# Reordering the head and the attention bursts of a fused attention and feed-forward kernel

## The chip, the cores and the metric

The kernel runs on one core of a Trainium2 chip. The metric is the device time of one execution in microseconds (us). One core has five engines that matter here: TensorE (matmul; PE in the profile, and PEld for its weight loads), VectorE (DVE), ScalarE (ACT), GpSimd (POOL, which here only issues loads that cast from f32 to bf16), and SyncE (SP, which here issues the stores of the output and the transposing transfers). Matmul results land in PSUM, eight banks of 128 x 512 f32; ACT and DVE read them out from there.

## The reference

The input is q, k, v of 8 batches x 12 heads x 448 positions x 64, and the weights of a feed-forward layer, 768 to 2048 to 768, with a slope alpha for each of the 2048.

```python
def _attn_ref(q, k, v):                       # (8, 12, 448, 64)
    scores = (1.0 / np.sqrt(64)) * np.matmul(q, k.transpose(0, 1, 3, 2))
    attn = np.maximum(scores, 0.0) ** 2 / 448
    return np.matmul(attn, v)

def _moe_ref(x, w_in, w_out, alpha):          # (3584, 768), (768, 2048), (2048, 768), (2048,)
    h = x @ w_in
    g = np.maximum(h, 0.0) + alpha * np.minimum(h, 0.0)
    return g @ w_out

# x is the attention output with the heads side by side: (8 * 448, 12 * 64)
```

## The kernel before

The work is cut into 24 "quads" of four heads (three quads to a batch) and each quad into seven "chunks" of 64 key positions. A chunk is four 64x64 matmuls into a pair of PSUM banks (`score_mm`), a relu out of PSUM on ACT or DVE, and a square in bf16 from SBUF to SBUF on DVE. When the seven chunks of a quad are squared, `attnv` multiplies them with v (28 matmuls). After three quads a batch has its input to FFN1 (`f1`: 16 outputs `ff`, six matmuls each over `km`, then `neg` on ACT and a multiply-add on DVE). Two batches share one FFN2 (`f2`: 7 row blocks `c` x 2 halves, 16 matmuls each, a copy out on ACT and two stores). The scores of later quads are mixed in between these. q and k are transposed either on TensorE (`turn_pe`, quads 0 to 5) or by a copy on DVE and a transposing transfer (`turn_dma`, from quad 6). Each engine works through its instructions in the order of this program; `take_pair` and `take_bank` hand out the PSUM banks that were taken longest ago.

```python
    raw_pool = ctx.enter_context(tc.tile_pool(name="raw", bufs=3))
    v_pool = ctx.enter_context(tc.tile_pool(name="v", bufs=7))
    perm_pool = ctx.enter_context(tc.tile_pool(name="perm", bufs=2))
    T_pool = ctx.enter_context(tc.tile_pool(name="T", bufs=4))
    rl_pool = ctx.enter_context(tc.tile_pool(name="rl", bufs=7))
    at_pool = ctx.enter_context(tc.tile_pool(name="at", bufs=12))
    xT_pool = ctx.enter_context(tc.tile_pool(name="xT", bufs=2))
    g_pool = ctx.enter_context(tc.tile_pool(name="g", bufs=1))
    neg_pool = ctx.enter_context(tc.tile_pool(name="neg", bufs=3))
    o_pool = ctx.enter_context(tc.tile_pool(name="o", bufs=4))
    # ... [cut: weights, identity, PSUM tile]
    def take_pair():
        lo = min((0, 2, 4, 6), key=lambda i: (max(taken[i], taken[i + 1]), i))
        take(lo, 2)
        return psum[:, lo:lo + 2]

    def take_bank():
        i = min(range(8), key=lambda i: (taken[i], i))
        take(i, 1)
        return psum[:, i]
    # ... [cut: loads; quad 0 is loaded ahead of the rest as f32 and cast on DVE and ACT]
    def turn_pe(n, cuts=((0, NJ, "D"),), cuts_k=((0, NJ, "D"),)):
        t = T_pool.tile([128, 2, NJ, 128], BF16, tag="T", name="T")
        for i, name in enumerate("qk"):
            src = raw.pop((n, name))
            for lo, hi, eng in (cuts, cuts_k)[i]:
                ps = take_bank().bitcast(BF16)
                for j in range(lo, hi):
                    for s in range(2):
                        nc.tensor.transpose(ps[64 * s:64 * s + 64, 128 * j:128 * j + 128], src[:, s, j], ident)
                dst = t[:, i, lo:hi].rearrange("p j c -> p (j c)")
                if eng == "D":
                    nc.vector.tensor_copy(dst, ps[:, 128 * lo:128 * hi])
                else:
                    nc.scalar.copy(dst, ps[:, 128 * lo:128 * hi])
        T[n] = t
    def turn_dma(n):
        p = perm_pool.tile([128, 2, NJ, 2, D], BF16, tag="perm", name="perm")
        for i, name in enumerate("qk"):
            nc.vector.tensor_copy(p[:, i], raw.pop((n, name)).rearrange("p s j d -> p j s d"))
        t = T_pool.tile([128, 2, NJ, 128], BF16, tag="T", name="T")
        nc.sync.dma_start_transpose(out=t.rearrange("p a j c -> p (a j) c"),
                                    in_=p.rearrange("p a j s d -> p (a j s d)"))
        T[n] = t
    def score_mm(n, j):
        ps = take_pair()
        t = T[n]
        for r in range(2):
            for c in range(2):
                nc.tensor.matmul(ps[64 * c:64 * c + 64, r, :S],
                                 t[64 * r:64 * r + 64, 1, j, 64 * c:64 * c + 64],
                                 t[64 * r:64 * r + 64, 0, :, 64 * c:64 * c + 64],
                                 start=True, stop=True)
        return ps

    def relu(ps, eng):
        rl = rl_pool.tile([128, 2, S], BF16, tag="rl", name="rl")
        if eng == "A":
            nc.scalar.activation(rl, ps[:, :, :S], ACTF.Relu)
        else:
            nc.vector.tensor_scalar(rl, ps[:, :, :S], 0.0, None, ALU.max)
        return rl

    def square(n, j, rl):
        a = at_pool.tile([128, 2, S], BF16, tag="at", name="at")
        nc.vector.tensor_tensor(a, rl, rl, ALU.mult)
        att[(n, j)] = a

    def attnv(n):
        ps = take_pair()
        vv = vraw.pop(n)
        for j in range(NJ):
            a = att.pop((n, j))
            for r in range(2):
                for s in range(2):
                    nc.tensor.matmul(ps[64 * s:64 * s + 64, r, :S],
                                     vv[64 * r:64 * r + 64, s, j, :],
                                     a[64 * r:64 * r + 64, s],
                                     start=(j == 0), stop=(j == NJ - 1))
        b, g = divmod(n, NG)
        if g == 0:
            xT[b] = xT_pool.tile([128, NG, 2, S], BF16, tag="xT", name="xT")
        if n < 2:
            nc.scalar.activation(xT[b][:, g], ps[:, :, :S], ACTF.Copy, scale=out_scale)
            return
        nc.scalar.activation(xT[b][:, g, 0], ps[:, 0, :S], ACTF.Copy, scale=out_scale)
        nc.vector.tensor_scalar(xT[b][:, g, 1], ps[:, 1, :S], out_scale, None, ALU.mult)

    late = []

    def sc(chunks):

        for n, j, eng in chunks:
            late.append((n, j, relu(score_mm(n, j), eng)))

    def sq(k=99):
        for g in late[:k]:
            square(*g)
        del late[:k]

    def run(chunks):
        sc(chunks)
        sq()
    def f1_mm(ps, b, ff, ks):
        for km in ks:
            nc.tensor.matmul(ps, w_in_sb[:, km // 2, km % 2, bass.ts(ff, 128)],
                             xT[b][:, km // 2, km % 2, :],
                             start=(km == 0), stop=(km == KM - 1))

    def f1_out(ps, b, ff):
        if b % 2 == 0 and ff == 0:
            gT[b // 2] = g_pool.tile([128, KF, 2 * S], BF16, tag="g", name="gT")
        neg = neg_pool.tile([128, S], F32, tag="neg", name="neg")
        nc.scalar.activation(neg, ps, ACTF.Relu, scale=-1.0)
        nc.vector.scalar_tensor_tensor(gT[b // 2][:, ff, (b % 2) * S:(b % 2) * S + S],
                                       neg, beta_sb[:, ff:ff + 1], ps, ALU.mult, ALU.add)
        sq(1)

    def f1(b, ff):
        ps = take_bank()[:, :S]
        f1_mm(ps, b, ff, range(KM))
        f1_out(ps, b, ff)

    def f2(sb, c, hf, parts=((0, HALF),)):
        o = o_pool.tile([128, HALF], F32, tag="o", name="osb")
        for lo, hi in parts:
            ps = take_bank()[:, :hi - lo]
            for ff in range(KF):
                nc.tensor.matmul(ps, gT[sb][:, ff, bass.ts(c, 128)], w_out_sb[:, hf, ff, lo:hi],
                                 start=(ff == 0), stop=(ff == KF - 1))
            nc.scalar.copy(o[:, lo:hi], ps)
            for u in range(2):
                blk = 2 * c + u
                b, j = 2 * sb + blk // NJ, blk % NJ
                rows = out[b * S:(b + 1) * S].rearrange("(pp j) d -> j pp d", j=NJ)
                eng = nc.scalar if u and hi - lo < HALF else nc.sync
                eng.dma_start(out=rows[j][:, hf * HALF + lo:hf * HALF + hi], in_=o[64 * u:64 * u + 64, lo:hi])
    # ... [the schedule: the head]
    pat = "ADAAAAA"

    def ch(n, lo, hi, p=pat):
        return [(n, j, p[j]) for j in range(lo, hi)]
    load_w_in(0)
    load_w_in(1)
    turn_pe(0, ((0, 4, "D"), (4, NJ, "D")), ((0, 2, "D"), (2, NJ, "D")))
    sc(ch(0, 0, 4))
    sq(3)
    load_qk(3)
    load_v(3)
    sc(ch(0, 4, 6))
    turn_pe(1)
    sc(ch(0, 6, 7))
    sq(4)
    load_w_in(2)
    load_w_in(3)
    sc(ch(1, 0, 3, "AAA"))
    attnv(0)
    load_qk(4)
    load_v(4)
    sq(2)
    sc(ch(1, 3, 4))
    turn_pe(2)
    sq(1)
    sc([(1, 4, "D"), (1, 5, "A"), (1, 6, "A")])
    sq(2)
    load_w_out(0)
    sc(ch(2, 0, 2, "AA"))
    sq(2)
    attnv(1)
    load_qk(5)
    load_v(5)
    load_w_out(1)
    sc(ch(2, 2, 4, "AAAAAAA"))
    nc.vector.tensor_scalar(beta_sb, alpha_sb, -1.0, 1.0, ALU.mult, ALU.add)
    sq(3)
    sc(ch(2, 4, 7, "AAAAADA"))
    sq()
    early = []
    for ff in range(2):
        ps = take_bank()[:, :S]
        f1_mm(ps, 0, ff, range(4))
        early.append(ps)
    attnv(2)
    for ff in range(2):
        f1_mm(early[ff], 0, ff, range(4, KM))
        f1_out(early[ff], 0, ff)
    def prepare(n):
        if n < NQ:
            turn_dma(n)
        if n + 2 < NQ:
            load_qk(n + 2)
            load_v(n + 2)
    # ... [cut: FFN1 of batch 0 with the chunks of quads 3 and 4, FFN2 c=0..2, quads 4 and 5]
    def some(k):
        lo = at_c[0]
        at_c[0] = min(lo + k, len(chunks))
        return [(n, j, e) for (n, j), e in zip(chunks[lo:at_c[0]], "ADA")]

    def burst(n):

        sc(some(3))
        attnv(n)
        sc(some(3))
        sq()
    for ff in range(KF):
        if ff < 4:
            f1_mm(early[ff], 1, ff, range(4, KM))
            f1_out(early[ff], 1, ff)
        else:
            f1(1, ff)
        if ff in (1, 5, 9):
            prepare(6 + ff // 4)
    f2(0, 3, 0)
    run(some(3))
    f2(0, 3, 1)
    f2(0, 0, 1)
    run(some(3))
    f2(0, 1, 1)
    run(some(3))
    f2(0, 2, 1)
    f2(0, 4, 0)
    prepare(9)
    burst(6)
    f2(0, 4, 1)
    f2(0, 5, 0)
    burst(7)
    f2(0, 5, 1)
    f2(0, 6, 0)
    prepare(10)
    burst(8)
    f2(0, 6, 1)

    for b in range(2, B):
        n0 = NG * (b + 1)
        last = b == B - 1
        sb = b // 2
        for ff in range(KF):
            if not last and ff == 8:
                run(some(3))
                prepare(n0 + 2)
            f1(b, ff)
        if b % 2 == 0:
            units = [(sb, c, h) for c in range(3) for h in range(2)]
            at = {1: 0, 3: 1, 5: 2}
        else:
            units = [(sb, c, h) for c in range(3, 7) for h in range(2)]
            at = {1: 0, 4: 1, 7: 2}
        for i, u in enumerate(units):
            if i in at and not last:
                g = at[i]
                if g != 1:
                    prepare(n0 + 3 + g // 2)
                burst(n0 + g)
            if last and i == len(units) - 1:
                f2(*u, parts=((0, 256), (256, HALF)))
            else:
                f2(*u)
```

## Time and profile before

| what | before |
|---|---|
| time of three runs, median (lowest to highest) | 392.98 us (392.55 to 398.75) |
| span of the profiled execution | 389.5 us |
| mean granted TensorE clock | 1.000 |
| busy share: PE, PEld, DVE, ACT, POOL | 97%, 55%, 68%, 53%, 17% |
| FFN2 matmuls (line 252) | 912, mean 323 ns in the record |
| FFN1 matmuls (line 229) | 768, mean 353 ns |
| relu on ACT (line 178), on DVE (line 180) | 120 of 928 ns, 48 of 1086 ns |
| square on DVE (line 185) | 168 of 618 ns |
| multiply-add of FFN1 on DVE (line 238), `neg` on ACT (line 237) | 128 of 678 ns, 128 of 546 ns |
| transposing transfers | 18, median 7.6 us from issue to landing |
| share of the DMA engines by stretches of 10 us | 0.99 to 1.30 up to 90 us, 0.00 to 1.20 after |

How to read it. A matmul's record runs from its start to a modelled end, and the next one starts long before that end; so the mean duration of a record is not what the matmul costs, and a PE that is busy for 97% is not a PE at its peak. What a stretch of matmuls costs is read from one start to the next in the timeline or in the chain of work that ended last. In the rows of groups, a name such as `rl<-psum` says which tile is written from which, `x120` how often; after the bar stand the engine's busy time in them, the mean duration of one in ns, and the idle time of that engine just before them with what ended it. A line of the timeline has the start, the time to the end of the last of the merged instructions, engine, line, operation, tiles and count. "idle before <-X" in brackets says that the engine had stood still and that X released it.

### The profile page before, as it was taken

The numbers are of one execution on the slowest core, as the hardware profiler recorded it, in microseconds if no ns is written. First come the engines' busy times: TensorE is split into PE (matmuls) and PEld (weight loads), VectorE is DVE, ScalarE is ACT, GpSimd is POOL, SyncE is SP. The second block draws the span as 40 slices with busy tenths as digits, with TensorE's granted clock in tenths as the row PEclk, the third lists the DMA queues.
The fourth block names the chain that finished last, engine by engine and source line by source line (L and its number), as shares of the span: only waits on it lengthen the run. The fifth ranks groups of instructions, "written<-read, shape, count | busy, mean of one in ns | idle before, by whom it ended". The sixth has DMA issues, their size and how long they took to land.

```text
span 389.5 us, 7956 instructions
## 1 busy us (share of the span) xinstructions
PE 378.2 (97%) x3228; PEld 216.0 (55%) x3228; DVE 263.9 (68%) x418; ACT 207.5 (53%) x332; POOL 65.5 (17%) x97
## 2 busy tenths in 40 slices
PE   7779999999999999999999999999999999999996
PEld 5435454555665556645655456654666546655564
DVE  3977966865777777868756687878756786735300
ACT  4966566545546546555455554655644565524311
POOL 7557212520202040202202022102000000000000
PEclk9999999999999999999999999999999999999999
DMA  9999999996859089574939259490832311120023
GB/s 181 191 202 204 206 211 206 167 195 139 134 86 144 29 129 169 82 98 73 159 89 146 55 53 176 95 153 8 164 82 51 80 24 46 42 61 2 12 72 82
DMA packets 71909, 43.75 MB, mean 112 GB/s; under 512 B 38208, under 2 KB 71872, under 8 KB 71872
## 3 DMA queue, kind: packets, MB, share of 16 engines
q0 software_dynamic: 27312, 23.04, 40.4%
q1 hardware_dynamic: 44128, 19.65, 25.7%
q8 instruction: 25, 0.41, 0.4%
q10 hardware_dynamic: 432, 0.56, 0.4%
q14 instruction: 12, 0.10, 0.1%
HBM read 47.00 MB, written 11.01 MB: 149 GB/s over the span
## 4 chain that ended last, share of the span: by engine, by line
PE 88%; ACT 5%; DVE 3%; issue 2%; DMA 1%; ACTq 0%
PE psum L252 38%; PE psum L229 36%; PE psum L169 7%; PE psum L195 6%; ACT rl L178 4%; DVE at L185 2%; DMA qfirst<-in_q_dram 1%; DVE T L147 1%; PE psum L144 1%; ACT xT L205 1%; DVE rl L180 1%; DVE gT L238 0%; ACT osb L254 0%; DVE qraw L127 0%; ACTq L260 0%
## 5 line engine op out<-in xcount | busy, mean ns | idle before, releaser
L252 PE MATMUL psum<-w_out_sb,gT 128*128 128x384 bf16 (+2 forms) x912 | 150.7, 323 | 0.2
L229 PE MATMUL psum<-xT,w_in_sb 128*128 128x448 bf16 x768 | 148.7, 353 | 1.1 <-ACT xT L205 0.6
L252 PEld LDWEIGHTS <-gT 128*128 128x128 bf16 x912 | 87.6, 98 | 61.5 <-issue 6.7
L229 PEld LDWEIGHTS <-w_in_sb 128*128 128x128 bf16 x768 | 74.2, 98 | 71.8 <-issue 4.4
L238 DVE SCALAR_TENSOR_TENSOR gT<-neg,beta_sb,psum 128x448 bf16<-128x448 f32 x128 | 84.5, 678 | 41.3 <-ACT neg L237 40.9
L237 ACT ACTIVATE neg<-psum 128x448 f32<-128x448 f32 x128 | 69.3, 546 | 70.3 <-PE psum L229 64.7
L178 ACT ACTIVATE rl<-psum 128x896 bf16<-128x896 f32 x120 | 102.9, 928 | 1.2 <-PE psum L169 1.2
L185 DVE TENSOR_TENSOR at<-rl 128x896 bf16<-128x896 bf16 x168 | 94.1, 618 | 3.5 <-ACT rl L178 3.4
L254 ACT COPY osb<-psum 128x384 f32<-128x384 f32 (+2 forms) x57 | 27.0, 474 | 97.5 <-PE psum L252 94.0
L180 DVE TENSOR_SCALAR rl<-psum 128x896 bf16<-128x896 f32 x48 | 52.1, 1086 | 37.1 <-PE psum L169 37.1
L91 POOL DMA_DIRECT2D qraw<-in_q_dram x24 | 17.2, 718 | 190.2 <-DVE perm L155 170.1
L169 PE MATMUL psum<-T 64*64 64x448 bf16 x672 | 44.7, 355 | 3.8 <-DVE T L147 1.4
L195 PE MATMUL psum<-at,vraw 64*64 64x448 bf16 x672 | 37.9, 351 | 0.7 <-ACT rl L178 0.2
L169 PEld LDWEIGHTS <-T 64*64 64x64 bf16 x672 | 20.9, 105 | 21.6 <-issue 14.6
L195 PEld LDWEIGHTS <-vraw 64*64 64x64 bf16 x672 | 24.8, 106 | 10.9 <-issue 3.7
L206 DVE TENSOR_SCALAR xT<-psum 128x448 bf16<-128x448 f32 x22 | 13.7, 625 | 14.3 <-PE psum L195 7.2
L91 POOL DMA_DIRECT2D kraw<-in_k_dram x24 | 17.3, 721 | 6.9 <-PE psum L169 3.3
L98 POOL DMA_DIRECT2D vraw<-in_v_dram x25 | 18.0, 722 | 1.2 <-DMA w_in_sb<-in_moe_w_in_dram 0.4
L205 ACT ACTIVATE xT<-psum 128x448 bf16<-128x448 f32 x22 | 12.0, 545 | 5.4 <-PE psum L195 5.4
L155 DVE COPY perm<-qraw 128x896 bf16<-128x896 bf16 x18 | 11.0, 612 | 0.4 <-DMA T<-perm 0.4
L108 POOL DMA_DIRECT2D w_in_sb<-in_moe_w_in_dram x16 | 10.0, 628 | 7.4 <-DMA vraw<-in_v_dram 2.5
L155 DVE COPY perm<-kraw 128x896 bf16<-128x896 bf16 x18 | 11.0, 609 | 0.0
(19 smaller groups left out, 35.5 us busy)
## 6 DMA issues: line engine op xcount, KB each, us to landing
out_dram<-osb SPq DMA_DIRECT2D x110, 96.0 KB, 2.3
vraw<-in_v_dram POOLq DMA_DIRECT2D x25, 224.0 KB, 7.4
qraw<-in_q_dram POOLq DMA_DIRECT2D x24, 224.0 KB, 4.8
kraw<-in_k_dram POOLq DMA_DIRECT2D x24, 224.0 KB, 6.7
w_in_sb<-in_moe_w_in_dram POOLq DMA_DIRECT2D x16, 192.0 KB, 8.7
w_out_sb<-in_moe_w_out_dram POOLq DMA_DIRECT2D x2, 1536.0 KB, 18.6
qfirst<-in_q_dram SPq DMA_DIRECT2D x1, 448.0 KB, 4.4
kfirst<-in_k_dram ACTq DMA_DIRECT2D x1, 448.0 KB, 4.7
```

The source lines that it names most:

```text
L91: nc.gpsimd.dma_start(out=t.rearrange("p m j d -> p m (j d)"), in_=flat[:, 2 * g:2 * g + 2])
L155: nc.vector.tensor_copy(p[:, i], raw.pop((n, name)).rearrange("p s j d -> p j s d"))
L169: nc.tensor.matmul(ps[64 * c:64 * c + 64, r, :S], t[64 * r:64 * r + 64, 1, j, 64 * c:64 * c + 64], t[64 * r:64 * r + 64, 0, :, 64 * c:64 * ...
L178: nc.scalar.activation(rl, ps[:, :, :S], ACTF.Relu)
L180: nc.vector.tensor_scalar(rl, ps[:, :, :S], 0.0, None, ALU.max)
L185: nc.vector.tensor_tensor(a, rl, rl, ALU.mult)
L195: nc.tensor.matmul(ps[64 * s:64 * s + 64, r, :S], vv[64 * r:64 * r + 64, s, j, :], a[64 * r:64 * r + 64, s], start=(j == 0), stop=(j == NJ ...
L229: nc.tensor.matmul(ps, w_in_sb[:, km // 2, km % 2, bass.ts(ff, 128)], xT[b][:, km // 2, km % 2, :], start=(km == 0), stop=(km == KM - 1))
L237: nc.scalar.activation(neg, ps, ACTF.Relu, scale=-1.0)
L238: nc.vector.scalar_tensor_tensor(gT[b // 2][:, ff, (b % 2) * S:(b % 2) * S + S], neg, beta_sb[:, ff:ff + 1], ps, ALU.mult, ALU.add)
L252: nc.tensor.matmul(ps, gT[sb][:, ff, bass.ts(c, 128)], w_out_sb[:, hf, ff, lo:hi], start=(ff == 0), stop=(ff == KF - 1))
L254: nc.scalar.copy(o[:, lo:hi], ps)
```

## The change

The change has five parts, and the arithmetic stays as it was.

1. **Head.** The first of the two copies that take the transposed k of quad 0 out of PSUM goes from DVE to ACT; the read-out of the second attention result (quad 1) is split between ACT and DVE as it already is for later quads; one square of quad 2 is done on ACT; three instead of two chunks of quad 2 come ahead of the A@V of quad 1; and the first four instead of the first two outputs of FFN1 are begun early, over the 512 rows of `w_in` whose input is there before quad 2 is finished. They stand half before and half after the A@V of quad 2, in PSUM banks that `hold` keeps out of the rotation until they are read. This is to keep ACT and DVE evenly loaded and TensorE at work while they catch up.
2. **Bursts.** A burst between two FFN2 blocks had three chunks, A@V, three chunks; now it has three, A@V, two.
3. **Plain triples.** The chunks that the bursts give up are done as a second plain group of three under each FFN1 (at outputs 6 and 12; before, one group at 8), and as a fourth plain group in the FFN2 of batch 0.
4. **Quad 8.** It was loaded twice; now it is loaded once.
5. **Transposing transfers.** `turn_dma` and the loads are called sooner, so that the transposed tiles are there for the earlier chunks.

```diff
@@ -75,6 +75,12 @@
         take(lo, 2)
         return psum[:, lo:lo + 2]
 
+    def hold():
+
+        i = min(range(8), key=lambda i: (taken[i], i))
+        taken[i] = 10**9
+        return i
+
     def take_bank():
         i = min(range(8), key=lambda i: (taken[i], i))
         take(i, 1)
@@ -180,9 +186,12 @@
             nc.vector.tensor_scalar(rl, ps[:, :, :S], 0.0, None, ALU.max)
         return rl
 
-    def square(n, j, rl):
+    def square(n, j, rl, eng="D"):
         a = at_pool.tile([128, 2, S], BF16, tag="at", name="at")
-        nc.vector.tensor_tensor(a, rl, rl, ALU.mult)
+        if eng == "A":
+            nc.scalar.activation(a, rl, ACTF.Square)
+        else:
+            nc.vector.tensor_tensor(a, rl, rl, ALU.mult)
         att[(n, j)] = a
 
     def attnv(n):
@@ -199,7 +208,7 @@
         b, g = divmod(n, NG)
         if g == 0:
             xT[b] = xT_pool.tile([128, NG, 2, S], BF16, tag="xT", name="xT")
-        if n < 2:
+        if n == 0:
             nc.scalar.activation(xT[b][:, g], ps[:, :, :S], ACTF.Copy, scale=out_scale)
             return
         nc.scalar.activation(xT[b][:, g, 0], ps[:, 0, :S], ACTF.Copy, scale=out_scale)
@@ -231,7 +240,7 @@
                              start=(km == 0), stop=(km == KM - 1))
 
     def f1_out(ps, b, ff):
-        if b % 2 == 0 and ff == 0:
+        if b // 2 not in gT:
             gT[b // 2] = g_pool.tile([128, KF, 2 * S], BF16, tag="g", name="gT")
         neg = neg_pool.tile([128, S], F32, tag="neg", name="neg")
         nc.scalar.activation(neg, ps, ACTF.Relu, scale=-1.0)
@@ -267,7 +276,7 @@
 
     load_w_in(0)
     load_w_in(1)
-    turn_pe(0, ((0, 4, "D"), (4, NJ, "D")), ((0, 2, "D"), (2, NJ, "D")))
+    turn_pe(0, ((0, 4, "D"), (4, NJ, "D")), ((0, 2, "A"), (2, NJ, "D")))
     sc(ch(0, 0, 4))
     sq(3)
     load_qk(3)
@@ -289,46 +298,58 @@
     sc([(1, 4, "D"), (1, 5, "A"), (1, 6, "A")])
     sq(2)
     load_w_out(0)
-    sc(ch(2, 0, 2, "AA"))
-    sq(2)
+    early = {}
+    todo = []
+
+    def some_early(count):
+        for ff, km in todo[:count]:
+            if ff not in early:
+                early[ff] = hold()
+            f1_mm(psum[:, early[ff], :S], 0, ff, (km,))
+        del todo[:count]
+
+    sc(ch(2, 0, 3, "AAA"))
+    sq(3)
     attnv(1)
     load_qk(5)
     load_v(5)
     load_w_out(1)
-    sc(ch(2, 2, 4, "AAAAAAA"))
+    todo = [(ff, km) for ff in range(4) for km in range(4)]
+    sc(ch(2, 3, 4, "AAAAAAA"))
     nc.vector.tensor_scalar(beta_sb, alpha_sb, -1.0, 1.0, ALU.mult, ALU.add)
-    sq(3)
+    sq(2)
     sc(ch(2, 4, 7, "AAAAADA"))
+    some_early(8)
+    square(*late.pop(-2), "A")
     sq()
-    early = []
-    for ff in range(2):
-        ps = take_bank()[:, :S]
-        f1_mm(ps, 0, ff, range(4))
-        early.append(ps)
     attnv(2)
-    for ff in range(2):
-        f1_mm(early[ff], 0, ff, range(4, KM))
-        f1_out(early[ff], 0, ff)
+    some_early(8)
+    for ff in range(4):
+        f1_mm(psum[:, early[ff], :S], 0, ff, range(4, KM))
+        f1_out(psum[:, early[ff], :S], 0, ff)
+        take(early[ff], 1)
 
 
     def f1s(b, lo, hi):
         for ff in range(lo, hi):
             f1(b, ff)
 
+    def load(n):
+        if n < NQ:
+            load_qk(n)
+            load_v(n)
+
     def prepare(n):
         if n < NQ:
             turn_dma(n)
-        if n + 2 < NQ:
-            load_qk(n + 2)
-            load_v(n + 2)
-
-    f1s(0, 2, 3)
+        load(n + 2)
+
     turn_pe(3)
     load_qk(6)
     load_v(6)
-    f1s(0, 3, 5)
+    f1s(0, 4, 6)
     sc(ch(3, 0, 3))
-    f1s(0, 5, 8)
+    f1s(0, 6, 8)
     sc(ch(3, 3, 6))
     f1s(0, 8, 10)
     turn_pe(4)
@@ -368,7 +389,7 @@
 
         sc(some(3))
         attnv(n)
-        sc(some(3))
+        sc(some(2))
         sq()
 
     early = []
@@ -384,25 +405,29 @@
             f1_out(early[ff], 1, ff)
         else:
             f1(1, ff)
-        if ff in (1, 5, 9):
-            prepare(6 + ff // 4)
+        if ff in (1, 4, 7):
+            turn_dma(6 + ff // 3)
+        if ff == 11:
+            load(9)
+            load(10)
     f2(0, 3, 0)
     run(some(3))
     f2(0, 3, 1)
     f2(0, 0, 1)
+    prepare(9)
     run(some(3))
     f2(0, 1, 1)
     run(some(3))
     f2(0, 2, 1)
+    run(some(3))
     f2(0, 4, 0)
-    prepare(9)
     burst(6)
     f2(0, 4, 1)
     f2(0, 5, 0)
+    prepare(10)
     burst(7)
     f2(0, 5, 1)
     f2(0, 6, 0)
-    prepare(10)
     burst(8)
     f2(0, 6, 1)
 
@@ -411,9 +436,10 @@
         last = b == B - 1
         sb = b // 2
         for ff in range(KF):
-            if not last and ff == 8:
+            if not last and ff in (6, 12):
                 run(some(3))
-                prepare(n0 + 2)
+            if not last and ff in (1, 9):
+                prepare(n0 + 2 + ff // 8)
             f1(b, ff)
         if b % 2 == 0:
             units = [(sb, c, h) for c in range(3) for h in range(2)]
@@ -424,8 +450,8 @@
         for i, u in enumerate(units):
             if i in at and not last:
                 g = at[i]
-                if g != 1:
-                    prepare(n0 + 3 + g // 2)
+                if g == 1:
+                    prepare(n0 + 4)
                 burst(n0 + g)
             if last and i == len(units) - 1:
                 f2(*u, parts=((0, 256), (256, HALF)))
```

## The prediction

> **What bounds the kernel now.** I read the page first, then the chain of work that ended last in order of time, then the busy time by stages, and last the timeline of the two places that the change touches.
>
> ```profile
> PE 378.2 (97%) x3228; PEld 216.0 (55%) x3228; DVE 263.9 (68%) x418; ACT 207.5 (53%) x332; POOL 65.5 (17%) x97
> PE 88%; ACT 5%; DVE 3%; issue 2%; DMA 1%; ACTq 0%
> PE psum L252 38%; PE psum L229 36%; PE psum L169 7%; PE psum L195 6%; ACT rl L178 4%; DVE at L185 2%; DMA qfirst<-in_q_dram 1%; DVE T L147 1%; PE psum L144 1%; ACT xT L205 1%; DVE rl L180 1%; DVE gT L238 0%; ACT osb L254 0%; DVE qraw L127 0%; ACTq L260 0%
> ```
>
> TensorE sets the end: 88% of the chain is matmuls, and the two feed-forward layers alone are 74%. None of these matmuls is removed. What the change can win is the other 12%, and within the 88% whatever PE loses when it turns from one kind of matmul to another. So I need the cost of a matmul, from the chain in order of time:
>
> ```profile
> 66.38 16.75 PE psum L229 x88
> 131.66 0.69 PE psum L169 x12
> 189.76 7.97 PE psum L252 x48
> ```
>
> FFN1: 16.75/88 = 0.190 us each. FFN2: 7.97/48 = 0.166 us with the turns, 2.60 us for a block of 16 in the undisturbed middle. A plain triple of chunks (12 matmuls) takes 0.69 us, of which some 0.1 is the turn back to full-size matmuls. Then the stages, with PE, DVE and ACT side by side:
>
> ```profile
> 7.20:31.00 23.80, 18.70 (x277) 10.11 (x278) 20.56 (x36) 18.48 (x24) 13.80 (x22) 1.00 1.24 198
> 31.00:49.20 18.20, 17.92 (x149) 8.60 (x146) 15.44 (x26) 12.44 (x21) 8.37 (x12) 1.00 1.29 204
> 213.70:256.70 43.00, 43.00 (x362) 24.88 (x360) 33.91 (x54) 24.19 (x39) 6.42 (x9) 1.00 0.63 100
> ```
>
> Only from 7.2 to 31 us is PE idle by its records (18.70 of 23.80 us), and there DVE (20.56) and ACT (18.48) are nearly full: the head is bound by relu and square. In the later periods PE never rests, and DVE has 9 us of air in 43.
>
> The timeline of the head's end shows the waits:
>
> ```profile
> 19.81 0.38 PE L195 MATMUL psum<-at,vraw 64*64 64x448 bf16 x4
> 20.24 0.92 ACT L203 ACTIVATE xT<-psum 128x896 bf16<-128x896 f32 x1 [0.33 <-PE psum L195]
> 21.06 3.34 ACT L178 ACTIVATE rl<-psum 128x896 bf16<-128x896 f32 x4
> 22.54 1.08 DVE L180 TENSOR_SCALAR rl<-psum 128x896 bf16<-128x896 f32 x1
> 22.83 1.67 PE L229 MATMUL psum<-xT,w_in_sb 128*128 128x448 bf16 x8 [0.43 <-ACT rl L178]
> 23.54 2.22 DVE L185 TENSOR_TENSOR at<-rl 128x896 bf16<-128x896 bf16 x4
> 24.43 1.77 PE L195 MATMUL psum<-at,vraw 64*64 64x448 bf16 x28
> 26.23 0.54 ACT L205 ACTIVATE xT<-psum 128x448 bf16<-128x448 f32 x1 [1.83 <-PE psum L195]
> 26.82 2.05 PE L229 MATMUL psum<-xT,w_in_sb 128*128 128x448 bf16 x10 [0.63 <-ACT xT L205]
> ```
>
> ACT stands 0.33 us for the A@V of quad 1, then reads it out whole, and only then begins four relus of quad 2; DVE squares the last four after that; the A@V of quad 2 waits for them; and FFN1 waits 0.63 us for its read-out. And a burst, in a later period:
>
> ```profile
> 237.31 0.80 PE L169 MATMUL psum<-T 64*64 64x448 bf16 x12
> 237.51 0.54 ACT L205 ACTIVATE xT<-psum 128x448 bf16<-128x448 f32 x1
> 238.11 5.36 PE L252 MATMUL psum<-w_out_sb,gT 128*128 128x384 bf16 x32
> ```
>
> The second triple of a burst takes 0.80 us to the next FFN2 block where a plain one takes 0.69. The rotation of banks gives that block a bank of the A@V, and ACT leaves it at 237.51+0.54 = 238.05; the block starts at 238.11. So 0.11 us of each burst is a wait.
>
> **What the skill says.** "TensorE: Matmul & The Clock Gate", section "Back-to-back issue gap", gives N/2.4 + 2.5 ns for a lone stream: 189 ns at N=448 and 162.5 at 384. The trace agrees (190; 2.60/16 = 162.5), so inside a run of matmuls nothing is left to win. "Perfetto Trace Analysis", section "Identifying the Most-Contended Engine", warns that matmul busy time is no measure of roofline; here the 97% hides the head's waits and the turns. "ScalarE: Activation LUTs", section "What ACT_TABLE_LOAD costs", has 186 ns + 0.833 ns an element, about 93 ns of it overlapped back to back. For 896 elements that is 0.93 us and 0.84; the relus are 928 ns alone and 3.34/4 = 0.84 in a row. No Square on ACT is in this trace; as an estimate from that page I take 0.85.
>
> **Part by part.**
>
> *Start of the head.* DVE's four copies of quad 0 take 1.28 us from 6.28, and the first score starts at 7.22. Moving the 256-column copy (281 ns) to ACT, free at 6.5 after its cast, lets that score start at about 7.05. ACT and DVE are both full from there to 20 us, so all of it moves by 0.17, say 0.2 us.
>
> *Quads 1 and 2.* With three chunks of quad 2 ahead of the A@V of quad 1, ACT doesn't stand: its relus run on to 19.7 + 0.85 = 20.55 (before, they ended at 19.9). Then half the read-out (0.54, to 21.1), relus of chunks 3, 4, 6 (to about 23.6), the Square (to 24.5). DVE: the last square of quad 1 to 19.55, one of quad 2, half the read-out 0.62, the constant 0.24, two squares, to about 21.95; its relu to 22.95; three squares, the last behind ACT's relu, to 24.65. The last part of the A@V starts at 24.75 instead of 25.82. PE in between: eight early FFN1 matmuls from 22.0, when the first held bank is free; the A@V from 23.6 to about 25.0; then eight more, 1.5 us, to 26.5. By then the read-out (25.15 to 25.8) is done, so the 0.63 us wait is hidden. The rest of FFN1 starts at 26.5 instead of 26.82, with 16 matmuls behind it instead of 8: 0.32 + 8 x 0.19 = 1.8 us won. This holds the 0.2 of the start.
>
> *To the first FFN2 block.* It stands at 49.2 now, so at 47.4. I expect at most 0.2 us lost: four multiply-adds now come ahead of the copies of quad 3's transposes on DVE, which end at about 31.15, when PE wants them at 31.27.
>
> *Bursts and plain triples.* A burst with two chunks behind takes 0.69 - 0.19 = 0.50 for its second part, and the FFN2 block takes a bank of the third chunk of the first triple, which ACT left at 235.88 + 1.73 = 237.61, before the 237.8 at which PE can use it: the 0.11 wait goes. The three chunks given up in a period (0.57 us) come back as a plain triple of 0.69 plus about 0.09 for the turn out of the full-size matmuls: 0.78. A period wins 3 x 0.11 and loses 0.21: 0.12 us. Where the period has eight FFN2 blocks, the first triple of two bursts also runs 0.05 to 0.09 long, so perhaps 0.2. Four periods give 0.65, the FFN2 of batch 0 another 0.12, the last period with scores about nothing: 0.75. Against this, DVE under FFN1 has 1.135 - 0.68 = 0.46 us of air per output, a triple adds 1.0 + 3 x 0.56 = 2.7 us and a `turn_dma` 1.14. Between outputs 6 and 12 both fall, and the bank of output 10, which output 12 takes, comes free about when it is wanted (8.1 after the first triple against 8.3). I take off 0.1 per period, 0.5 in all. Left: 0.3 us.
>
> *Quad 8 and the transfers.* They take 0.67 MB of loads away around 60 to 70 us. No PE wait there is on a DMA, so I count nothing.
>
> Sum: 1.8 - 0.1 + 0.3 = 2.0 us. From 392.98: 391.0; as the three times of before lie nearer 392.6 than their highest, I say 390.8.
>
> **The rivals.**
>
> *FFN2 finds its weights late.* The first half of `w_out` is issued at 31.24 and lands 15.0 us later, at 46.24, behind a DMA that is full (share 1.24 to 1.29); an earlier head doesn't bring it. That leaves 1.2 us before 47.4. The transposes of quad 4 want a k that lands at 37.45 and get to it at about 37.9. If the loads slip by more, the head's gain falls to 0.5 to 1.0 us and the time is 392. Against it: both have room.
>
> *DVE becomes the bound under FFN1.* With two triples and two `turn_dma` a period DVE may hold banks past the time PE wants them. At 0.5 us a triple this costs 4 us over six periods and eats everything: 393 to 395. For it: the short reuse of outputs 10 to 12 and, in the head, of 4 to 6. Against it: by stages DVE has 9 us of air, and one triple at output 8 showed no wait.
>
> *The whole head gain is swallowed.* If quad 2's A@V waits for DVE anyway, only the hidden wait and the early matmuls that fall into idle time count: about 1.0 us, 391.8.
>
> **Range and chances.** The middle is 390.8. Everything won in the head, nothing lost under FFN1 gives 389.5; DVE in the way gives 392.8. Two per cent are 7.9 us, more than all of PE's waits in the head that I can find, so faster by 2% has 0.02; slower by 2% needs a wait of over 1.3 us in each of six periods: 0.02.
>
> **What would show it.** Right: the first score near 7.05; FFN1 matmuls on both sides of the A@V of quad 2; the first FFN2 block near 47.4; second parts of bursts at 0.5 us with no wait on the read-out; periods of 42.9 and 48.1 us from FFN1 to FFN1 against 43.0 and 48.3. Wrong: an FFN2 start held by a DMA, PE waits on the multiply-add behind the second triple, or a longer period.

## The result, and the profile after

The changed kernel takes 389.78 us (median of 4 executions, 389.69 to 390.1), against 393.24 us (392.55 to 398.75) for the kernel before beside it: ratio 0.9919, 95% interval 0.99 to 0.9939. In every comparison here the ratio leaves out executions that lie over 1.5% above the fastest of their kernel, while medians and ranges are of all executions.

Two numbers do not fit together at first sight: the medians are 3.5 us apart, the traced spans only 1.5 us (389.5 before, 388.0 after). Both are right, and the experiments are about this difference.

First the trace. The first line is the engine line of the page after, the second is its chain of waits by engine:

```profile
PE 378.4 (98%) x3228; PEld 210.6 (54%) x3228; DVE 266.2 (69%) x422; ACT 203.8 (53%) x329; POOL 63.3 (16%) x94
PE 90%; DVE 5%; ACT 2%; DMA 1%; issue 1%; ACTq 0%
```

As many matmuls as before, PE on the chain for 90% instead of 88%. ACT fell from 5% to 2% of the chain and DVE rose from 3% to 5%: of what PE has to wait for, more is now DVE's. The timeline of the head's end after the change (start, length, engine, line, operation; in brackets the idle time before it and what ended it):

```profile
20.60 2.73 ACT L184 ACTIVATE rl<-psum 128x896 bf16<-128x896 f32 x3
...
21.76 1.67 PE L238 MATMUL psum<-xT,w_in_sb 128*128 128x448 bf16 x8 [0.43 <-ACT rl L184]
...
22.99 1.17 ACT L192 ACTIVATE at<-rl 128x896 bf16<-128x896 bf16 x1
23.37 1.52 PE L204 MATMUL psum<-at,vraw 64*64 64x448 bf16 x28
24.82 3.20 PE L238 MATMUL psum<-xT,w_in_sb 128*128 128x448 bf16 x16
24.92 0.55 ACT L214 ACTIVATE xT<-psum 128x448 bf16<-128x448 f32 x1 [0.76 <-PE psum L204]
```

Eight early FFN1 matmuls run while ACT and DVE work at the last relus and squares (21.76), eight more while quad 2 is read out: in the group of 16 at 24.82 the first eight are early ones, and PE runs straight through the read-out (24.92 + 0.55 = 25.47) that it used to wait 0.63 us for. FFN1 goes on without a break from 24.82; before, it went on only at 26.82, after that wait.

The windows of the first and a later stage with PE, DVE and ACT side by side (stretch, length, then busy time and count of PE, PEld, DVE, ACT, POOL; last the granted clock, DMA share and GB/s):

```profile
6.97:24.82 17.85, 14.51 (x233) 7.64 (x233) 17.25 (x30) 16.76 (x21) 9.69 (x16) 1.00 1.24 194
...
212.03:255.08 43.05, 43.05 (x362) 24.00 (x361) 34.51 (x55) 23.33 (x38) 6.42 (x9) 1.00 0.64 109
```

In the head DVE is now busy 17.25 of 17.85 us and has almost no air left. The last line is the six-block period from FFN1 to FFN1: 43.05 us, PE busy throughout.

The starts of the same work in both traces show where the 1.5 us come from:

| Start of | before | after | difference |
|---|---|---|---|
| first score | 7.22 | 6.97 | −0.25 |
| A@V of quad 2 | 24.43 | 23.37 | −1.06 |
| first FFN2 block | 49.21 | 47.40 | −1.81 |
| FFN1 of batch 1 | 62.96 | 61.13 | −1.83 |
| FFN1 of batch 2 | 122.42 | 120.67 | −1.75 |
| FFN1 of batch 3 | 165.40 | 163.72 | −1.68 |
| FFN1 of batch 5 | 256.72 | 255.08 | −1.64 |
| end | 389.5 | 388.0 | −1.5 |

The head wins 1.8 us, and from there on 0.3 is given back, in the periods with the new bursts and plain triples. That explains the traces. The other 2 us of the medians are in no row of this table: they come from executions that the one trace of the kernel before is not.

### The profile page after: what moved, and what is told of

It is laid out like the page before. It is cut to its first block, busy times and chain, and to the rows that moved or that the text cites. A ratio compares the mean times of both kernels' runs of the same rounds, so it can differ in the third digit from the quotient of the medians.

```text
span 388.0 us, 7917 instructions
## 1 busy us (share of the span) xinstructions
PE 378.4 (98%) x3228; PEld 210.6 (54%) x3228; DVE 266.2 (69%) x422; ACT 203.8 (53%) x329; POOL 63.3 (16%) x94
## 3 DMA queue, kind: packets, MB, share of 16 engines
q1 hardware_dynamic: 44128, 19.65, 23.6%
## 4 chain that ended last, share of the span: by engine, by line
PE 90%; DVE 5%; ACT 2%; DMA 1%; issue 1%; ACTq 0%
PE psum L261 38%; PE psum L238 35%; PE psum L204 8%; PE psum L175 8%; DVE at L194 2%; ACT rl L184 2%; DMA qfirst<-in_q_dram 1%; DVE gT L247 1%; PE psum L150 1%; DVE T L153 1%; DVE rl L186 1%; ACT neg L246 0%; ACT osb L263 0%; DVE qraw L133 0%; ACTq L269 0%
## 5 line engine op out<-in xcount | busy, mean ns | idle before, releaser
L261 PEld LDWEIGHTS <-gT 128*128 128x128 bf16 x912 | 86.7, 98 | 63.1 <-issue 8.6
L247 DVE SCALAR_TENSOR_TENSOR gT<-neg,beta_sb,psum 128x448 bf16<-128x448 f32 x128 | 83.1, 676 | 29.5 <-ACT neg L246 29.5
L184 ACT ACTIVATE rl<-psum 128x896 bf16<-128x896 f32 x115 | 99.7, 934 | 0.5 <-PE psum L175 0.5
L186 DVE TENSOR_SCALAR rl<-psum 128x896 bf16<-128x896 f32 x53 | 57.5, 1086 | 40.3 <-PE psum L175 40.2
L175 PE MATMUL psum<-T 64*64 64x448 bf16 x672 | 45.9, 356 | 2.4 <-ACT rl L184 0.9
L204 PEld LDWEIGHTS <-vraw 64*64 64x64 bf16 x672 | 23.9, 106 | 11.4 <-issue 3.2
L175 PEld LDWEIGHTS <-T 64*64 64x64 bf16 x672 | 18.0, 105 | 22.1 <-issue 15.6
L97 POOL DMA_DIRECT2D kraw<-in_k_dram x23 | 16.5, 719 | 7.8 <-PE psum L175 4.8
```

The lines of the kernel that those rows point to most:

```text
L97: nc.gpsimd.dma_start(out=t.rearrange("p m j d -> p m (j d)"), in_=flat[:, 2 * g:2 * g + 2])
L175: nc.tensor.matmul(ps[64 * c:64 * c + 64, r, :S], t[64 * r:64 * r + 64, 1, j, 64 * c:64 * c + 64], t[64 * r:64 * r + 64, 0, :, 64 * c:64 * ...
L204: nc.tensor.matmul(ps[64 * s:64 * s + 64, r, :S], vv[64 * r:64 * r + 64, s, j, :], a[64 * r:64 * r + 64, s], start=(j == 0), stop=(j == NJ ...
```

## The experiments

Twelve kernels, in three groups, the kernel before run beside each group on the same chip (393.13 us over 59 executions, 391.19 to 403.14, beside the first four; 393.09 over 55 beside the next four; 392.59 over 27 beside the last four). The first theory was the prediction's: head −1.8, bursts a little, loads nothing. The rivals: the bursts or the loads carry part of the gain.

### The kernel before again

An unchanged copy, for the spread.

> The kernel before, unchanged, timed against itself. Its traced span was 389.5 us, 1.5 us above that of the changed kernel (388.0), but its timed median is 3.5 us above. If the difference is a wait that before has in most executions and did not have in the traced one, this profile or its times show it: spans of 390.7 us or more in most executions, and somewhere in the first 130 us a stage longer than in the first trace. If it is mere scatter, the times lie between 391 and 393.5 us and no stage differs.

392.64 us over 22 executions, ratio 0.9993 (0.9962 to 1.0024). Its executions lie anywhere from 391.19 to 401.04. Of its 22 spans 13 are 390.7 us or more, as the theory of a wait had it. The one that was traced has 391.6, 2.1 above the first trace, and all of that stands in its head already: the first FFN2 block begins at 51.36 instead of 49.21 (see "What stays open" below). So the kernel before has a floor near 391.2 and a tail of up to 10 us, while the changed kernel's 4 executions lie within 0.4. Floor against floor the gain is 391.19 − 389.69 = 1.5 us, which is what the traces say.

### The head alone

The kernel before with the head of the change (first part of the diff) and nothing else.

```diff
-    turn_pe(0, ((0, 4, "D"), (4, NJ, "D")), ((0, 2, "D"), (2, NJ, "D")))
+    turn_pe(0, ((0, 4, "D"), (4, NJ, "D")), ((0, 2, "A"), (2, NJ, "D")))
...
-    sc(ch(2, 0, 2, "AA"))
-    sq(2)
+    sc(ch(2, 0, 3, "AAA"))
+    sq(3)
     attnv(1)
...
+    some_early(8)
+    square(*late.pop(-2), "A")
     sq()
     attnv(2)
+    some_early(8)
```

> Before with the reordered head alone. Theory (the head is nearly all of the gain that a trace shows): first FFN2 block at 47.4 us instead of 49.2, everything after it in step, 1.8 us less than before by the trace, about 391.2 us; and if the rest of the timed gain is a wait on loads or transposing transfers, it stays at 391.2. Rival (the head gives all 3.2 us in the timed runs, because what varies lies there): 389.8 us.

397.67 us (392.82 to 399.11, 6 executions), ratio 1.0113 (1.0047 to 1.0179): the part that wins 1.8 us in the trace makes the kernel *slower* when it is alone, and neither 391.2 nor 389.8 came. Its first FFN2 block stands at 47.7, so the gain of the head is there; it is lost later. The timeline of this kernel in the FFN2 of batch 0, in its best execution:

```profile
81.41 1.79 PE L261 MATMUL psum<-w_out_sb,gT 128*128 128x384 bf16 x10
...
82.19 0.62 DVE L161 COPY perm<-qraw 128x896 bf16<-128x896 bf16 x1 [6.13 <-DMA T<-perm]
...
83.97 0.34 PE L261 MATMUL psum<-w_out_sb,gT 128*128 128x384 bf16 x1 [0.78 <-DVE gT L247]
84.01 1.73 ACT L246 ACTIVATE neg<-psum 128x448 f32<-128x448 f32 x3 [5.27 <-DVE gT L247]
```

Read it from the `perm` line: DVE stands 6.13 us before the `perm` copy of quad 8, because `perm` has two buffers and the transposing transfer of quad 6, which reads the older one, is not finished. DVE works in order, so the multiply-adds of FFN1 behind the copy stand too; ACT stands 5.27 us for them, and PE comes to the end of the `gT` that it has. The FFN2 block that begins at 81.41 takes 5.79 us instead of 2.69.

The same place was there to read in the trace of before, and I passed over it:

```profile
66.72 0.72 POOL L91 DMA_DIRECT2D qraw<-in_q_dram  x1 [6.63 <-DMA qraw<-in_q_dram]
...
71.41 17.28 SPq L157 DMA_TRANSPOSE T<-perm  x3
...
78.03 0.62 DVE L155 COPY perm<-qraw 128x896 bf16<-128x896 bf16 x1 [0.41 <-DMA T<-perm]
```

The first line begins the second load of quad 8; its k and v follow, to 69.7. It is issued 1.7 to 4.7 us before the transposing transfer of quad 6 (71.41), and its k and v land at 72.4 and 74.0, when that is under way. DVE waited 0.41 us here, which cost nothing. In this execution the transfer landed 6.5 us after its issue; in the traces of other kernels with the second load it takes up to 13.9.

### The bursts alone

The kernel before with bursts of three and two, the extra plain triples (that in the FFN2 of batch 0 is not shown here), and the calls of `prepare` that go with them; the loads of quad 6 to 8 and the call for quad 9 stay as before.

```diff
-        sc(some(3))
+        sc(some(2))
         sq()
...
-            if not last and ff == 8:
+            if not last and ff in (6, 12):
                 run(some(3))
-                prepare(n0 + 2)
+            if not last and ff in (1, 9):
+                prepare(n0 + 2 + ff // 8)
```

> Before with the bursts of three and two chunks and the plain triples alone, quad 8 loaded twice and the transposing transfers of quads 6 to 9 called as before. Theory (this part is worth nothing): by the trace the six stages with bursts lose 0.3 us together, so 393.0 to 393.5 us. Rival (the rest of the timed gain is here): 391.5 us.

397.14 us (394.37 to 409.64, 22 executions), ratio 1.0096 (1.0065 to 1.0126). No execution came near the floor of before, so there is a cost in all of them. The timeline shows it, at burst 7:

```profile
107.83 3.20 SPq L157 DMA_TRANSPOSE T<-perm  x1
115.68 0.42 PE L169 MATMUL psum<-T 64*64 64x448 bf16 x4
...
119.67 0.59 PE L169 MATMUL psum<-T 64*64 64x448 bf16 x4 [3.56 <-DMA T<-perm]
...
120.19 7.81 PE L252 MATMUL psum<-w_out_sb,gT 128*128 128x384 bf16 x32
```

With only two chunks behind the A@V, and a plain triple more before it, quad 9 is wanted sooner than before: 7.9 us after its transposing transfer was issued. That took 11.8 us, and PE waited 3.56 for the fifth chunk of the burst. The stop costs more than its length. The windows before, in and after it (PEclk is the third number from the end):

```profile
107.80:115.60 7.80, 7.80 (x88) 4.86 (x82) 6.58 (x11) 3.88 (x7) 3.22 (x5) 1.00 1.15 151
115.60:120.20 4.60, 1.04 (x17) 0.22 (x9) 0.62 (x1) 1.64 (x3) 0.00 (x0) 0.80 1.32 154
120.20:128.00 7.80, 7.80 (x40) 3.87 (x40) 3.77 (x6) 0.48 (x1) 0.00 (x0) 0.68 0.98 149
```

After the stop the granted clock is 0.68 for 7.8 us, and 32 matmuls take 7.8 us instead of 5.3. "TensorE: Matmul & The Clock Gate", section "Part 1: The HAM clock gate (the "warmup" mystery)", of the Trainium skill says that after an idle window of about 3.4 us the array runs at half rate until it has been busy for about as long. The trace agrees on the half rate (the weight loads stand 0.32 us apart from 120.49 to 124.97, where a matmul at full clock takes 0.166), but the time is longer: 7.8 us at a mean of 0.68 are 5.0 us at half rate and 2.8 at full. So some 2.5 us are lost after the 3.56. In the FFN2 of batch 0 this execution also has the wait of the head alone, 5.9 us on DVE, and the block at 82.97 takes 5.71 us.

### The loads alone

The kernel before with quad 8 loaded once, the transposing transfers of quads 6 to 8 called at outputs 1, 4, 7, and that of quad 9 three FFN2 blocks sooner (the recorded text for the last group of runs says two). The loads of quads 9 and 10 are called later than before, at output 11, but they start when their buffers come free: the first at 71.15 us, against 71.10 before.

```diff
-        if ff in (1, 5, 9):
-            prepare(6 + ff // 4)
+        if ff in (1, 4, 7):
+            turn_dma(6 + ff // 3)
+        if ff == 11:
+            load(9)
+            load(10)
...
+    prepare(9)
     run(some(3))
     f2(0, 1, 1)
...
-    prepare(9)
     burst(6)
```

> Before with quad 8 loaded once and the transposing transfers of quads 6 to 9 called sooner, nothing else. Theory (the rest of the timed gain is a wait of VectorE or of the queue of stores behind late loads of quad 8, which comes and goes between executions): 391.4 to 391.7 us and steadier than before. Rival (no wait there is on the path, as I predicted): 393.2 us as before.

391.43 us (391.24 to 392.0, 22 executions), ratio 0.9956 (0.9932 to 0.9979). The floor is that of before; what is gone is the tail. This is the part that I had counted as nothing, and it is worth 1.7 us of the median (393.13 − 391.43). DVE still waits for the transposing transfer, but not so long that it shows on PE:

```profile
78.55 0.62 DVE L155 COPY perm<-qraw 128x896 bf16<-128x896 bf16 x1 [2.58 <-DMA T<-perm]
```

So 2.58 us of waiting on DVE is hidden, and 5.9 or 6.1 is not.

### Which of the loads' parts: quad 8 once, or the calls sooner

The first theory had fallen. The new one: the second load of quad 8 makes the transposing transfer of quad 6 late, and the lateness reaches PE through DVE's wait for a `perm` buffer. The rivals: the sooner calls do it, or the number of buffers does. First the second load alone left out:

```diff
-        if n + 2 < NQ:
+        if n + 2 < NQ and n != 6:
```

> Before with the second load of quad 8 left out (it is loaded once, as in the changed kernel), the transposing transfers called as before. Theory (the second load, issued at 66.7 to 69.7 us, lands on top of the transposing transfer of quad 6 and makes it late, VectorE's copy for quad 8 waits in order for that transfer because there are two perm buffers, and TensorE stands when it waits over 3 us): the transfer of quad 6 lands in about 7 us, VectorE waits under 1 us, 391.4 us and steady. Rival (calling the transfers sooner is what helps): 393.1 us and as scattered as before.

391.71 us (391.19 to 393.84, 22 executions), ratio 0.9976 (0.9953 to 1.0). No execution is above 393.84, but 7 of 22 are above 392.3. The loads alone had none of 22 there, on another chip; so the sooner calls may still take away this rest, and that is not settled.

Then the calls sooner, with quad 8 still loaded twice:

```diff
-        if ff in (1, 5, 9):
-            prepare(6 + ff // 4)
+        if ff in (1, 4, 7):
+            prepare(6 + ff // 3)
```

> Before with the transposing transfers of quads 6 to 8 called at outputs 1, 4 and 7 instead of 1, 5 and 9, quad 8 still loaded twice. Theory: no help, VectorE only reaches the same wait some 2.3 us sooner and stands longer, so 393.5 to 396 us. Rival (sooner calls are what helps): 391.4 us.

392.42 us (391.52 to 396.41, 14 executions), ratio 0.9991 (0.9954 to 1.0029). The execution that was traced took 396.41, and its timeline has the same wait, longer:

```profile
84.51 0.62 DVE L155 COPY perm<-qraw 128x896 bf16<-128x896 bf16 x1 [8.66 <-DMA T<-perm]
...
86.30 3.96 PE L252 MATMUL psum<-w_out_sb,gT 128*128 128x384 bf16 x14 [3.23 <-DVE gT L238]
```

The sooner calls do not remove the collision. The median lies below the expected 393.5 to 396, and the highest execution is 396.41, where 18 of the 55 executions of the kernel before beside it lie above 397, so some help in the tail is not excluded. With the second load gone nothing is above 393.84.

### The buffer of the copy

If DVE's wait for a `perm` buffer is the path by which the transfer reaches PE, a third buffer must cut it.

```diff
-    perm_pool = ctx.enter_context(tc.tile_pool(name="perm", bufs=2))
+    perm_pool = ctx.enter_context(tc.tile_pool(name="perm", bufs=3))
```

> Before with three perm buffers instead of two, nothing else. Theory: VectorE's copy for quad 8 no longer waits for the transfer of quad 6, the late transfer is hidden, 391.4 us and steady although quad 8 is loaded twice. Rival (TensorE waits for the late transposed tile itself, or the stores behind it hold ScalarE): 393 us, scattered.

Before with three buffers: 391.74 us (391.33 to 396.19, 22 executions), ratio 0.999 (0.9963 to 1.0018). The median improves (393.09 beside it), the best does not, and the tail is shorter rather than gone: none of 22 above 397, against 18 of 55. By the ratio no difference is shown. On the head alone, with the same edit, the effect is larger:

> The reordered head alone, as in the run that took 397.7 us, but with three perm buffers. Theory (the head brings VectorE 1.8 us sooner to a copy that waits for the transposing transfer of quad 6, whose landing is timed by the loads and not by the head; so VectorE stands longer): with the third buffer no copy waits, and the head shows its own gain: 389.7 to 390.5 us. Rival (TensorE would wait for the late transposed tile or for a store anyway): 395 us or more.

Head alone and three buffers: 391.99 us (389.65 to 396.07, 14 executions), ratio 0.9974 (0.994 to 1.0008). One buffer brings 397.67 down by 5.7 us (1.0113 to 0.9974 as ratios), so DVE's wait is most of the path. It is not all of it: 389.7 to 390.5 was expected. In the traced execution PE itself waits for a transfer; a line of its timeline:

```profile
95.99 0.57 PE L175 MATMUL psum<-T 64*64 64x448 bf16 x8 [2.03 <-DMA T<-perm]
```

Here the transfer of quad 7 landed 22.6 us after its issue and cut a triple, begun at 93.57, in two. A buffer moves the wait; it does not take away what makes the transfer late.

### What makes it late: the second load

The head alone, with one line more:

```diff
-        if n + 2 < NQ:
+        if n + 2 < NQ and n != 6:
```

> The reordered head with quad 8 loaded once, two perm buffers, transposing transfers called as before. Theory (the second load of quad 8 is what makes the transfer of quad 6 late): 389.7 to 390.5 us. Rival (the sooner calls are needed as well): 392 us or more, scattered.

389.52 us (389.47 to 389.98, 6 executions), ratio 0.9935 (0.9917 to 0.9953), against 397.67 with the load. One condition in one line is worth about 8 us of this kernel's median (about 7 by the ratios, 0.9935 instead of 1.0113, each against the kernel before on its own chip), and beside the head no other part of the change is needed. DVE's wait for the transfer is 1.0 us in its trace, and the transfer of quad 6 landed in 7.1 us:

```profile
76.78 0.62 DVE L161 COPY perm<-qraw 128x896 bf16<-128x896 bf16 x1 [0.97 <-DMA T<-perm]
```

The transposing transfer of quad 6 and the wait at the `perm` copy of quad 8, over the traces with two buffers:

| Kernel | transfer lands after, us | DVE waits, us |
|---|---|---|
| before | 6.5 | 0.4 |
| before again | 7.7 | 1.6 |
| head alone | 12.2 | 6.1 |
| bursts alone | 12.0 | 5.9 |
| calls sooner, quad 8 twice | 13.1 | 8.7 |
| bursts alone, quad 9 sooner | 11.2 | 8.8, in two waits |
| loads alone | 7.0 | 2.6 |
| quad 8 once | 7.1 | 1.0 |
| head, quad 8 once | 7.1 | 1.0 |
| changed kernel, bursts of before | 6.6 | 2.7, in two |
| changed kernel | 7.0 | 2.6 |
| changed kernel again | 7.0 | 4.4, in two |

With one load it is 6.6 to 7.1 us; with two it is what comes, from 6.5 to 13.1. This holds for quad 6 only: the transfer of quad 7 took 15.2 to 17.0 us in the traces with one load as well (10.5 to 19.9 with two).

How the second load makes the transfer late is less clear than that it does. The loads of quad 9 start beside the transfer of quad 6 in either case (69.28 against 69.59 us in the trace of the head with quad 8 once). And with two loads the issue times do not decide it: in the bursts alone and with the calls sooner, the second load of quad 8, the loads of quad 9 and the transfer of quad 6 were issued within 0.2 us of their times in the trace of before, and the transfer took 12.0 and 13.1 us instead of 6.5.

### The bursts, with the rest right

The changed kernel with the bursts, the triples and their calls of before (the edit of the bursts alone, in reverse):

```diff
-        sc(some(2))
+        sc(some(3))
...
-            if not last and ff in (6, 12):
+            if not last and ff == 8:
```

> The changed kernel with the bursts and plain triples of before: head and loads alone. Theory (by the traces the bursts of three and two chunks cost 0.3 us over the six stages): 389.5 us, 0.3 less than the changed kernel. Rival (the shorter bursts keep other waits away): above 389.8 us.

389.64 us (389.46 to 390.05, 10 executions), ratio 0.9917 (0.9886 to 0.9947); its traced span is 387.8. So without the new bursts the kernel is at least as fast.

The bursts alone with the transfer of quad 9 called three FFN2 blocks sooner:

```diff
     f2(0, 0, 1)
+    prepare(9)
     run(some(3))
...
-    prepare(9)
     burst(6)
```

> The shorter bursts alone, with the transposing transfer of quad 9 called where the changed kernel calls it, two FFN2 blocks sooner; quad 8 still loaded twice. In the run without this, TensorE stood 3.6 us for that transfer in the second burst. Theory: this wait is gone, the one for the copy of quad 8 stays as in before, so 392 to 394 us, scattered like before. Rival (the bursts themselves lose the time): 396 us or more.

393.31 us (391.4 to 401.86, 14 executions), ratio 1.0021 (0.9992 to 1.005). The wait of 3.56 us at burst 7 is gone (best 391.4 instead of 394.37), the tail of before is there. So that sooner call is what the shorter bursts need, not a gain of its own.

> The changed kernel once more, for a narrower interval. Theory: 389.8 us, without scatter, 1.5 us below the fastest executions of before (391.2) and 3.3 below their median; 0.15 us above the version with head and loads but the bursts of before (389.64).

The changed kernel once more: 390.0 us (389.76 to 390.14, 6 executions), ratio 0.9945 (0.9927 to 0.9962). Head and quad 8 once (389.52), beside it on the same chip, needs nothing of the rest and lies 0.5 us lower. I recommend that version: it has the lowest median of all and a shorter diff than the changed kernel with the bursts of before, from which its time (0.1 us less, on another chip) cannot be told apart.

## Why the prediction was right and where it was wrong

**The head: right, to 0.1 us.** The first FFN2 block was predicted at 47.4 and stands at 47.40. The A@V of quad 2 was to run from 23.6 to 25.0 and ran from 23.37 to 24.89; with eight early matmuls behind it the rest of FFN1 begins about 24.82 + 8 x 0.19 = 26.34, for a predicted 26.5. The start came at 6.97 for 7.05. Square on ACT, estimated at 0.85 us, cost 0.83: its record is 1.17 us long, but it begins before the relus ahead of it end (20.60 + 2.73 = 23.33), and it ends at 22.99 + 1.17 = 24.16. The rival "The whole head gain is swallowed", with about 1.0 us won, did not come in this trace. The loss of up to 0.2 us that I had allowed for the copies of quad 3's transposes did not come there (they end at 31.02, the scores start at 31.23). One of that size is to be seen around the first FFN2 block:

```profile
46.67 0.67 DVE L247 SCALAR_TENSOR_TENSOR gT<-neg,beta_sb,psum 128x448 bf16<-128x448 f32 x1
...
47.39 0.81 PE L261 MATMUL psum<-w_out_sb,gT 128*128 128x384 bf16 x4
```

The triple ahead of it began at 46.52 and took 0.87 us to this block, where it took 0.69 before: PE is held about 0.18 us until DVE's multiply-add ends at 46.67 + 0.67 = 47.34. The rival "FFN2 finds its weights late" did not come: `w_out` was there at 46.2.

**The bursts: the wait went, the gain did not come.** The sum had 0.75 from the structure less 0.5 for DVE: +0.3 us. Measured is −0.27 (offset −1.83 at FFN1 of batch 1, −1.56 at that of batch 7). A burst in a later period of the changed kernel:

```profile
244.16 0.61 PE L175 MATMUL psum<-T 64*64 64x448 bf16 x8
244.36 0.54 ACT L214 ACTIVATE xT<-psum 128x448 bf16<-128x448 f32 x1
...
244.70 1.47 PE L261 MATMUL psum<-w_out_sb,gT 128*128 128x384 bf16 x8
```

FFN2 begins at 244.70 while the read-out runs to 244.90: the wait on the read-out is gone, as predicted. But from the second part to FFN2 it is 244.70 − 244.16 = 0.54 us, not 0.50. That is 0.26 less than before (0.80), of which 0.19 is the chunk that was taken away: a burst wins 0.07, not 0.11. Three make 0.21 a period, one plain triple more costs 0.22 (0.69 and 0.10 for the turn, less 0.57; predicted 0.21), and the first triple of the first burst takes 0.64 instead of 0.59. A period of six blocks thus goes from 42.98 to 43.05 us, where 42.9 was predicted, one of eight from 48.34 to 48.31, where 48.1 was predicted. The 0.5 for DVE under FFN1 was not needed: in the six-block period FFN1 ran without a stop between its two triples. "DVE becomes the bound" did not come.

**The loads: this is the step that failed.** "Quad 8 and the transfers. They take 0.67 MB of loads away around 60 to 70 us. No PE wait there is on a DMA, so I count nothing." The statement on PE's waits was true of the trace, and the conclusion was wrong for the kernel. The loads alone are worth 1.7 us of the median, because a transfer that was in time in the one trace is late in others, and it reaches PE through DVE's copy and DVE's multiply-adds, where I had looked only for a PE wait on a DMA. The traces of the head alone, the bursts alone and the calls sooner show this path; no execution of the kernel before that lost time in this way was itself traced. In the changed kernel that wait was larger than in the one trace of before, and still hidden:

```profile
76.67 0.62 DVE L161 COPY perm<-qraw 128x896 bf16<-128x896 bf16 x1 [2.58 <-DMA T<-perm]
```

The number also said it before any trace: three executions with 392.55, 392.98 and 398.75 are not a kernel at its floor. I used them to lower the prediction by 0.2 and asked no further.

**The sum.** Predicted 390.8, between 389.5 and 392.8; measured 389.78, inside it. The head gave 1.8, the bursts took 0.3, and 2.0 of the 3.5 us between the medians is left over (1.1 of 2.6 when the changed kernel ran again). That rest is put down to the missing second load, because the loads alone take away 1.7 and the scatter with it; it is a remainder and not a wait read from a trace of the kernel before. So the reasons that I gave cover less than half to somewhat over half of the gain, and that the time fell inside the range is in part luck. The head also pays only when the transfer is kept in time: alone it is 1.0113, without the second load 0.9935.

**What stays open.** The kernel before, and before with three buffers, show a second source of scatter: the first loads of quad 1 land late. In the unchanged copy this is the whole excess of the traced execution; its wait at the `perm` copy, 1.6 us, was hidden. The timeline of the unchanged copy, at its head:

```profile
10.62 0.58 PE L144 MATMUL psum<-ident,qraw 128*64 128x128 bf16 x14 [1.04 <-DMA qraw<-in_q_dram]
```

There the first FFN2 block stands at 51.36 instead of 49.21, and from 12.5 to 20 us the granted clock is 0.81. With three buffers the block stands at 50.84. The traces of the steady kernels do not have it (the longest such wait is 0.22 us), and no run explains why. How much of the scatter of the kernel before comes from here and how much from the second load was not separated. The executions of quad 8 once that lie above 392.3 may be this; they were not traced. Why the head alone is worse than the kernel before is open too. It begins the second load of quad 8 1.8 us before the transfer of quad 6 (68.05 and 69.84), where the kernel before has 4.7 between them (66.72 and 71.41); that this matters is an argument, not a run.

## What to carry to other kernels

Before counting a DMA change as nothing, look for the narrowest place behind it: an in-order engine that waits even 0.4 us for a transfer's buffer is a warning, since that transfer may take twice as long in the next execution and everything queued behind the wait stops too. Compare the lowest time as well as the median over many executions: the lowest shows what the instruction stream is worth, the distance between them what luck with transfers costs. And when compute is pulled forward, ask which transfer is now wanted sooner; taking away a needless load there came before the reordering could pay.

## What the hardware showed that I had not expected

- The transposing transfer of the same 14 blocks of a quad landed between 6.4 and 13.9 us after its issue (quad 6, all traces), and 22.6 us once (quad 7). With no second load beside it, it was 6.6 to 7.1 for quad 6, but 15.2 to 17.0 for quad 7.
- A stop of PE costs more than itself: 3.56 us of waiting was followed by 7.8 us at a granted clock of 0.68, another 2.5 us. The length of one stop does not decide it alone: in the head of the unchanged copy, waits of 1.04 and 0.51 us were followed by 0.81 from 12.5 to 20 us. Granted clocks of whole executions follow the time loosely: in the unchanged copy 0.999 to 1.0 up to 392.8 us, 0.99 at 398.4 and 0.987 at 401.0, but 1.0 at 394.8 as well.
- Records on ACT overlap in a row: the three relus before the Square are 1.11 to 1.14 us long in the record and start 0.80 us apart, and the Square of 1.17 us ends 0.83 after the last of them. The length of a record there is not what the instruction costs.
